# Attention heads as 64x64 tiles of TensorE, and the first activation in one ScalarE instruction

## The chip, the cores and the metric

One core of a Trainium2 chip runs the whole program. A core has TensorE (PE; its weight loads are listed as PEld), VectorE (DVE), ScalarE (ACT), GpSimd (POOL) and the queue that issues most DMAs, SyncE (SP). The metric is device time of one execution in microseconds (us); lower is better.

## The reference

For 8 batches of 8 heads (576 tokens, head width 64) linear attention is computed, then two pairs of dense layers with different activations. The attention's output is rearranged to 4608 tokens of 512 features.

```python
q_s = exp(q - max(q, -1)); q_s /= sum(q_s, -1) + 1e-9      # per token and head
k_s = exp(k - max(k, 2));  k_s /= sum(k_s, 2) + 1e-9       # per head, over its 576 tokens
kv  = einsum('bhsd,bhse->bhde', k_s, v)                    # 64x64 for each head
x   = einsum('bhsd,bhde->bhse', q_s, kv)                   # -> (4608, 512)
h = x @ w_in;   g = h / (1 + exp(-1.702 * h));  x1 = g @ w_out      # 512 -> 2048 -> 512
h2 = x1 @ w2_in; g2 = piecewise quadratic of h2;  out = g2 @ w2_out
```

## The kernel before, in words

A product in full precision is made of three products of rounded parts (high x high, high x low, low x high, type fp32r); `split` (L106) makes the parts: ScalarE copies the high part (L107), VectorE subtracts it (L108).

**Stage 0** is the part that the change touches. It has nine blocks `j` of 512 tokens, each of 16 steps `m`; step `s = 16j + m` is one call of `gemm1` (L794): 12 matmuls of 128x512 (L803 to L805) that give 128 rows of `h` for 512 tokens. Two steps fill a pair of PSUM banks `hps`; there are two such pairs, used in turn. After each second step `act` (L807) takes the pair: ScalarE computes tanh(0.851 h) (L812), VectorE (tanh + 1) * h (L813), which is twice the activation, and SP stores it to `g0` (L816). The factor 0.5 is put into the next stage's copies out of PSUM (`keep`, L396, and `more`, L401).

Beside the steps, `chain` (L824) lays out the attention of the next block. For each of four pairs of heads `hp`: `k_max`, `k_col`, `k_sub` (column maximum by two PE transposes, L681 and L688, and VectorE's subtraction, L691), `k_exp` (L700), and `k_v` (L702): ten fp32 matmuls (each is recorded as two) of a key chunk against [v, 1]; four chunks have 128 rows, the last has 64 (`n = P if r < KR else KT`). The two heads of a pair go to two halves of the array's columns. ScalarE writes the result, divided by the sums, as two 64x64 blocks on the diagonal of a 128x128 tile `kv` (L724); the rest of the tile is zero. For each of four tiles of 128 tokens `t`: `q1`, `q1e`, `q2` (softmax of q, L729 to L755), `q3` (four PE transposes, L764, and a copy, L769), and `q4` (L771): for each pair of heads a 128x128 fp32 matmul `px` per batch that the block reaches into (L774; blocks 1 to 7 reach into two), and `split` of `px` into the parts of `x`.

The first weight matrix is read as 64-bit floats and converted in block 0 itself, one piece `w(m)` of 128 columns for each step: `load_w` (L604), `conv_w` (L610; L92 on ScalarE, L94, L97, L101 on VectorE, then `split`). Later in the stage the other three matrices are converted and stored. **Stages 1 to 3** (`out_pass`, L359; `pass_in`, L485; `out_pass` again) are matmuls on data in DRAM.

What sets the order: the kernel is written as a list of jobs, each with a place in units of steps (`put`, `at`; Q3 and Q4, L46 and L47), sorted and called after each step. The framework then arranges the instructions of each engine by a model of their times, keeping all dependences, and each engine runs its list strictly in order.

## Time and profile before

| what | us |
|---|---|
| time, median of three runs | 1572.76 (1572.35 to 1576.16) |
| the profiled execution's own time | 1570.93 |
| its span, first to last instruction | 1569.1 |
| PE busy in the span | 1536.9 (98%) |
| DVE busy | 1163.6 (74%) |
| ACT busy | 821.9 (52%) |
| first matmul of step 0 begins at | 40.11 |

A busy matmul time counts the tail of a matmul while the next runs already, so what one costs is read from the distance between starts: undisturbed 128x512 matmuls start 0.227 us apart. A window of time shows all engines' busy time in it, the granted clock of TensorE (1.00 is 2.4 GHz, 0.50 is 1.2 GHz) and the load of the DMA engines.

### The profile page before, as it was taken

Reading aid. Unit: us, or ns where it says so; the run is one execution under the profiler, and the core shown is the slowest. Engines: PE = TensorE matmul, PEld = TensorE weight load, DVE = VectorE, ACT = ScalarE, POOL = GpSimd, SP = SyncE. Lnnn points to the kernel's source line nnn. Section 1 sums busy time; section 2 is a strip of 40 time slices with the busy share of each in tenths; the row PEclk is TensorE's granted clock in tenths of the full one; section 3 lists DMA queues with packets and bytes.
Section 4 is the critical chain, followed back from the end, with each engine's and each line's share of the span. In section 5 each row is a group of like instructions: output and inputs, shape, how many; then the busy total and the mean of one; then the engine's idle time right before and its main releaser. Section 6 shows DMA issues by size and latency. Waiting matters only on the chain. (4 is left out here: it accounts for less than half of the span.)

```text
span 1569.1 us, 20971 instructions
## 1 busy us (share of the span) xinstructions
PE 1536.9 (98%) x7748; PEld 1307.6 (83%) x7748; DVE 1163.6 (74%) x1546; ACT 821.9 (52%) x1058; POOL 8.8 (1%) x45
## 2 busy tenths in 40 slices
PE   4999999999999999999999999999999999999998
PEld 2677788777787888888999888888999888888998
DVE  6999887787843678686778577777664879696885
ACT  5555445544523444444445687778776544343442
POOL 0000000000000000000000000000000000000000
PEclk8999999999999999999999999999999999999999
DMA  8787788887787751615268766566744963535341
GB/s 234 212 258 266 263 271 274 267 271 252 251 293 274 289 201 68 213 56 178 71 199 310 294 223 241 202 231 228 259 160 169 426 201 136 159 110 144 111 121 41
DMA packets 249080, 330.65 MB, mean 211 GB/s; under 512 B 129553, under 2 KB 193041, under 8 KB 246289
## 3 DMA queue, kind: packets, MB, share of 16 engines
q1 hardware_dynamic: 243696, 328.09, 62.0%
q10 hardware_dynamic: 5280, 1.21, 0.4%
q8 instruction: 61, 1.00, 0.3%
q14 instruction: 43, 0.34, 0.1%
HBM read 190.84 MB, written 138.41 MB: 210 GB/s over the span
## 5 line engine op out<-in xcount | busy, mean ns | idle before, releaser
L107 ACT ACTIVATE s<-s 128x1024 fp32r<-128x1024 f32 (+2 forms) x363 | 325.1, 901 | 377.9 <-PE z L359 149.7
L108 DVE TENSOR_TENSOR s<-s,s 128x1024 fp32r<-128x1024 f32 (+2 forms) x363 | 369.0, 1023 | 152.7 <-PE zx L359 66.1
L359 PE MATMUL z<-s,w 128*128 128x512 f32 (+1 forms) x1920 | 399.8, 367 | 0.4 <-DVE s L108 0.4
L359 PEld LDWEIGHTS z<-s,w 128*128 128x128 f32 x1920 | 349.5, 188 | 45.9 <-DVE s L108 0.8
L359 PE MATMUL zx<-s,w 128*128 128x512 f32 (+1 forms) x1440 | 300.8, 367 | 0.7 <-DVE s L377 0.7
L359 PEld LDWEIGHTS zx<-s,w 128*128 128x128 f32 x1440 | 262.2, 188 | 34.6 <-DVE s L377 1.0
L803 PE MATMUL hps<-xh,w 128*128 128x512 f32 x576 | 236.2, 410 | 3.0 <-ACT w L107 3.0
L805 PE MATMUL hps<-xh,w 128*128 128x512 f32 x576 | 226.9, 394 | 0.7 <-DVE w L108 0.6
L804 PE MATMUL hps<-xl,w 128*128 128x512 f32 x576 | 226.2, 393 | 0.0
L121 DVE TENSOR_TENSOR s<-s,s 128x1024 f32<-128x1024 f32 (+2 forms) x196 | 204.7, 1058 | 12.7 <-DMA s<-g 8.9
L485 PE MATMUL z<-s,w 128*128 128x512 f32 (+1 forms) x960 | 207.2, 367 | 0.0
L485 PEld LDWEIGHTS z<-s,w 128*128 128x128 f32 x960 | 175.0, 188 | 22.9 <-DVE s L501 0.4
L485 PE MATMUL zx<-s,w 128*128 128x512 f32 (+1 forms) x720 | 158.5, 368 | 1.8 <-DVE s L121 1.6
L485 PEld LDWEIGHTS zx<-s,w 128*128 128x128 f32 x720 | 130.7, 188 | 20.8 <-DVE s L121 3.8
L813 DVE SCALAR_TENSOR_TENSOR sg<-sg,hps 128x1024 f32<-128x1024 f32 x72 | 87.7, 1218 | 62.2 <-ACT sg L812 59.6
L803 PEld LDWEIGHTS hps<-xh,w 128*128 128x128 f32 x576 | 108.8, 189 | 28.8 <-ACT w L107 4.3
L805 PEld LDWEIGHTS hps<-xh,w 128*128 128x128 f32 x576 | 108.2, 188 | 25.6 <-DVE w L108 2.4
L812 ACT ACTIVATE sg<-hps 128x1024 f32<-128x1024 f32 x72 | 73.8, 1025 | 101.4 <-PE hps L805 96.8
L804 PEld LDWEIGHTS hps<-xl,w 128*128 128x128 f32 x576 | 108.5, 188 | 20.9 <-issue 0.6
L500 ACT ACTIVATE s<-s 128x1024 f32<-128x1024 f32 (+1 forms) x80 | 77.6, 971 | 1.6
L499 ACT ACTIVATE s<-s,half 128x1024 f32<-128x1024 f32 (+1 forms) x40 | 42.4, 1060 | 23.6 <-DVE s L121 23.6
L501 DVE SCALAR_TENSOR_TENSOR s<-s,s 128x1024 f32<-128x1024 f32 (+1 forms) x40 | 44.7, 1117 | 12.6 <-ACT s L500 11.2
(79 smaller groups left out, 1074.2 us busy)
## 6 DMA issues: line engine op xcount, KB each, us to landing
s<-g SPq DMA_DIRECT2D x96, 512.0 KB, 5.1
g<-sg SPq DMA_DIRECT2D x72, 512.0 KB, 3.2
w<-wp_out SPq DMA_DIRECT2D x14, 2048.0 KB, 14.8
g<-s SPq DMA_DIRECT2D x48, 512.0 KB, 3.0
s<-g SPq DMA_DIRECT2D x48, 384.0 KB, 4.0
wp_out<-w SPq DMA_DIRECT2D x28, 512.0 KB, 4.0
wp_in<-w SPq DMA_DIRECT2D x28, 512.0 KB, 3.7
w<-wp_in SPq DMA_DIRECT2D x7, 2048.0 KB, 8.7
```

Of the source, the lines that this page charges most:

```text
L107: first = nc.scalar.activation(out=hi, in_=src, func=ACTF.Copy)
L108: return nc.vector.tensor_tensor(out=lo, in0=src, in1=hi.bitcast(FP32), op=ALU.subtract), first
L121: return nc.vector.tensor_tensor(out=o, in0=x, in1=y, op=op)
L359: nc.tensor.matmul(out=z[:, m, :n], lhsT=a, rhs=b[:, c, :], start=(p in OPENS and i == 0 and c == 0 and x == 0), stop=(i == 3 and c == 1 a ...
L485: nc.tensor.matmul(out=z[:, m, :n], lhsT=a, rhs=b[:, c, :], start=(p in OPENS and c == 0 and x == 0), stop=(c == 1 and x == 2), skip_group ...
L500: nc.scalar.activation(out=t, in_=t, func=ACTF.Square)
L501: nc.vector.scalar_tensor_tensor(out=t, in0=h, scalar=1.0, in1=t, op0=ALU.max, op1=ALU.min)
L803: nc.tensor.matmul(out=hps, lhsT=wh, rhs=xh[:, kk, :], start=(kk == 0), stop=False)
L804: nc.tensor.matmul(out=hps, lhsT=wh, rhs=xl[:, kk, :], start=False, stop=False)
L805: nc.tensor.matmul(out=hps, lhsT=wl, rhs=xh[:, kk, :], start=False, stop=(kk == KD - 1))
L812: nc.scalar.activation(out=sg, in_=hps, func=ACTF.Tanh, scale=0.851)
L813: nc.vector.scalar_tensor_tensor(out=sg, in0=sg, scalar=1.0, in1=hps, op0=ALU.add, op1=ALU.mult)
```

## The change

Four things change in stage 0. (1) `q4` handles two pairs of heads at once: per batch four matmuls of 64x64 tiles, one in each quarter of the array (`tile_position`), for four heads; `kv` holds the 64x64 blocks alone, and the rows of the first weight matrix are loaded in another order (two DMAs instead of one for each piece) so that the features fit. (2) In `k_v` all chunks have 128 rows; the rows that the last one lacks hold zeros (v) and exponentials of the lowest number (k). The result leaves PSUM by one activation instead of two. (3) ScalarE's function `Gelu_apprx_sigmoid` computes h*sigmoid(1.702h) in one instruction, and VectorE's instruction falls away, as do the factors 0.5 later. (4) Exponentials and that function are not in the same table of ScalarE, so the exponentials of two tiles of keys and two of queries are put together (EX), an extra order (`in_turn`) keeps ScalarE from mixing them with activations, and the places of the jobs behind them move (KV, Q3, Q4).

```diff
+    EX = (5, 5, 9, 9)
+    KV = (6, 7, 10, 11)
-    Q3 = (6.5, 8.5, 10.5, 12)
-    Q4 = (12.4, 13.2, 14, 14.8)
+    Q3 = (7.5, 8.5, 11.5, 12.5)
+    Q4 = (13.1, 14)
...
-                after(nc.scalar.activation(out=t, in_=z, func=ACTF.Copy, scale=1.0 if ph else 0.5), True)
+                after(nc.scalar.activation(out=t, in_=z, func=ACTF.Copy), True)
...
-                if ph:
-                    after(tt(t, t, z, ALU.add))
-                else:
-                    nc.vector.scalar_tensor_tensor(
-                        out=t, in0=z, scalar=0.5, in1=t, op0=ALU.mult, op1=ALU.add
-                    )
+                after(tt(t, t, z, ALU.add))
...
-        kv_t = [vpool.tile([P, HP, P], FP32, name=f"kv{i}") for i in range(2)]
+        kv_t = [vpool.tile([P, HP, D], FP32, name=f"kv{i}") for i in range(2)]
...
+            src = w1_in[:, m * P:(m + 1) * P].rearrange("(c k d) f -> c d k f", c=2, k=KD)
+            for c in range(2):
+                nc.sync.dma_start(
+                    out=raw1(m)[c * D:(c + 1) * D].rearrange("d (k f) -> d k f", k=KD), in_=src[c]
+                )
...
+        def in_turn(ins):
+            if st.get("turns"):
+                behind(ins, st.get("turn"))
+            st["turn"] = ins
...
-            nc.scalar.activation(out=kt, in_=kt, func=ACTF.Exp)
+            in_turn(nc.scalar.activation(out=kt, in_=kt, func=ACTF.Exp))
...
-                n = P if r < KR else KT
...
-                        lhsT=kt[:n, r, h, :],
-                        rhs=vt[:n, r, h, :],
+                        lhsT=kt[:, r, h, :],
+                        rhs=vt[:, r, h, :],
...
-            for j in range(2):
-                o = slice(j * D, (j + 1) * D)
-                nc.scalar.activation(out=kv[o, hp, o], in_=pk[o, :D], func=ACTF.Copy, scale=rs[o])
+            nc.scalar.activation(out=kv_t[b % 2][:, hp, :], in_=pk[:, :D], func=ACTF.Copy, scale=rs)
...
-        def q4(j, hp):
-            px = ps_a.tile([P, TB], FP32, tag="a", name="px")
+        def q4(j, pair):
+            px = [ps_a.tile([P, TB], FP32, tag="a", name="px") for _ in range(2)]
             for off, n, b, s in segs(j * TB, TB, S):
-                nc.tensor.matmul(
-                    out=px[:, off:off + n],
-                    lhsT=kv_t[b % 2][:, hp, :],
-                    rhs=st["qT", j][:, hp, off:off + n],
-                    start=True,
-                    stop=True,
-                )
+                for c in range(2):
+                    for r in range(2):
+                        rows = slice(r * D, (r + 1) * D)
+                        nc.tensor.matmul(
+                            out=px[r][c * D:(c + 1) * D, off:off + n],
+                            lhsT=kv_t[b % 2][rows, pair + 2 * c, :],
+                            rhs=st["qT", j][rows, pair + 2 * c, off:off + n],
+                            start=True,
+                            stop=True,
+                            tile_position=(r * D, c * D),
+                            skip_group_check=True,
+                        )
             xh, xl = x_sb[j]
-            split(xh[:, hp, :], xl[:, hp, :], px)
+            for r in range(2):
+                split(xh[:, 2 * pair + r, :], xl[:, 2 * pair + r, :], px[r])
...
-            nc.scalar.activation(out=sg, in_=hps, func=ACTF.Tanh, scale=0.851)
-            nc.vector.scalar_tensor_tensor(
-                out=sg, in0=sg, scalar=1.0, in1=hps, op0=ALU.add, op1=ALU.mult
-            )
+            in_turn(nc.scalar.activation(out=sg, in_=hps, func=ACTF.Gelu_apprx_sigmoid))
...
-                    put(2 * i + 3, k_exp, b, i)
-                    put(2 * i + 5, k_v, b, i)
+                    put(EX[i] + 0.3, k_exp, b, i)
+                    put(KV[i], k_v, b, i)
...
-                put(2 * i + 3.3, q1e, t)
-                put(2 * i + 5.2, q2, t)
+                put(EX[i], q1e, t)
+                put(KV[i] + 0.2, q2, t)
                 put(Q3[i], q3, t)
-                put(Q4[i], q4, j, i)
+                if i < 2:
+                    put(Q4[i], q4, j, i)
...
-        for t in kv_t:
-            nc.gpsimd.memset(t, 0.0)
+            nc.gpsimd.memset(t[KT:, KR, :, :D], 0.0)
```

How this moves instructions is seen in the lists of the engines. The line numbers in the lists of the changed kernel are its own: its L813 to L815 are the three matmuls of `gemm1`, L711 `k_v`, L768 `q3`, L781 `q4`, L684 and L691 the two transposes of `k_max`'s chain, L703 and L746 the exponentials of keys and queries, L822 the activation, L723 the copy of `kv`, L773 that of `q3`, L109 `split`'s first instruction, L94 and L169 conversions of later weights.

PE before, block 3, from the end of step 11 to the start of step 13 (most of the twelve matmuls of step 12 are left out):

```order
L805 MATMUL hps<-xh,w 128x512
L709 MATMUL pk<-v_303,kt 64x65 x10
L803 MATMUL hps<-xh,w 128x512
L804 MATMUL hps<-xl,w 128x512
...
L764 MATMUL pt<-ident,qt 128x128 x4
L774 MATMUL px<-qT,kv_305 128x256
L803 MATMUL hps<-xh,w 128x512
L804 MATMUL hps<-xl,w 128x512
L774 MATMUL px<-qT,kv_304 128x256
```

The same engine in the changed kernel, block 3, from the end of step 13:

```order
L815 MATMUL hps<-xh,w 128x512
L711 MATMUL pk<-v_302,kt 64x65 x10
L711 MATMUL pk<-v_303,kt 64x65 x10
L768 MATMUL pt<-ident,qt 128x128 x8
L813 MATMUL hps<-xh,w 128x512
L781 MATMUL px<-qT,kv_305 64x256 x4
L814 MATMUL hps<-xl,w 128x512
...
L781 MATMUL px<-qT,kv_304 64x256 x4
```

Two `k_v`, two `q3` and the first `q4` now stand together, at the start of step 14, where each stood at a step of its own from step 10 to step 13.

ACT before, block 3, from the tanh after step 9 to the one after step 11 (kv, qT, xh: copies out of PSUM):

```order
L812 ACTIVATE sg<-hps 128x1024
L107 ACTIVATE w<-w 128x512 x3
L724 ACTIVATE kv_304<-pk,rs 64x64 x2
L769 ACTIVATE qT<-pt 128x4x128
L107 ACTIVATE w<-w 128x512
L812 ACTIVATE sg<-hps 128x1024
```

ACT in the changed kernel, block 3, from the activation after step 9 to the one after step 11:

```order
L822 ACTIVATE sg<-hps 128x1024
L723 ACTIVATE kv_304<-pk,rs 128x64
L746 ACT_TABLE_LOAD
L746 ACTIVATE qt<-qt 128x512
L773 ACTIVATE qT<-pt 128x4x128
L94 ACTIVATE w<-w 128x1024
...
L746 ACTIVATE qt<-qt 128x512
L703 ACTIVATE kt<-kt 128x640 x2
L822 ACT_TABLE_LOAD
L822 ACTIVATE sg<-hps 128x1024
```

Between two activations ScalarE now has two loads of a table and four exponentials, with copies and conversions between them; there are 34 loads in the list where there was one.

DVE in the changed kernel, block 0, ahead of the weights of step 8 (kt is `k_sub`, qz and the last qt are `q2`, rs follows `k_v`; L96, L99, L103, L110 are the conversion of w(8) and its `split`):

```order
L721 TENSOR_SCALAR rs<-pk 128x1
L686 TENSOR_REDUCE mc<-pa 128x1
L722 RECIPROCAL rs<-rs 128x1
L753 TENSOR_REDUCE qz<-qt 128x8
L96 TENSOR_SCALAR w<-w 128x512
L757 TENSOR_SCALAR qz<-qz 128x8
L694 TENSOR_TENSOR kt<-kr,pb 128x640
L99 SCALAR_TENSOR_TENSOR w<-w 128x512
L758 RECIPROCAL qz<-qz 128x8
L103 SCALAR_TENSOR_TENSOR w<-w 128x512
L759 TENSOR_TENSOR qt<-qt,qz 128x512
L110 TENSOR_TENSOR w<-w 128x512
```

The first of them waits for the `k_v` that PE has at the start of step 8, and `k_sub` for a transpose that PE has behind it; the weights of step 8 stand behind both.

## Rows read from the trace of the kernel before

**Rows 1.** Windows: block 0 of stage 0, then its blocks 1 to 8.

```profile
core 0: us, PE busy (x) PEld busy (x) DVE busy (x) ACT busy (x) POOL busy (x), PEclk, DMA share, GB/s
40.10:101.30 61.20, 57.56 (x315) 43.22 (x314) 59.41 (x120) 35.59 (x59) 0.80 (x4) 1.00 0.78 234
101.30:523.00 421.70, 421.50 (x2281) 336.18 (x2280) 316.07 (x560) 194.40 (x292) 4.43 (x20) 1.00 0.80 268
```

**Rows 2.** Windows with line L803 alone (four to a step): blocks 0 and 1.

```profile
40.10:101.30 61.20, 27.14 (x65) 12.26 (x65) 1.00 0.78 234
101.30:156.00 54.70, 26.88 (x64) 12.15 (x64) 1.00 0.79 259
```

**Rows 3.** Timeline of PE: one q4 (start us, length us, line, tiles).

```profile
201.75 0.39 PE L804 MATMUL hps<-xl,w 128*128 128x512 f32 x1
201.97 0.39 PE L805 MATMUL hps<-xh,w 128*128 128x512 f32 x1
202.20 1.02 PE L774 MATMUL px<-qT,kv 128*128 128x192 f32 x4
202.82 0.63 PE L803 MATMUL hps<-xh,w 128*128 128x512 f32 x1
203.29 0.40 PE L804 MATMUL hps<-xl,w 128*128 128x512 f32 x1
```

**Rows 4.** Timeline of PE: one k_v.

```profile
248.15 0.39 PE L804 MATMUL hps<-xl,w 128*128 128x512 f32 x1
248.37 0.39 PE L805 MATMUL hps<-xh,w 128*128 128x512 f32 x1
248.69 0.95 PE L709 MATMUL pk<-v,kt 128*64 128x65 f32 x20
249.57 0.50 PE L803 MATMUL hps<-xh,w 128*128 128x512 f32 x1
249.91 0.39 PE L804 MATMUL hps<-xl,w 128*128 128x512 f32 x1
```

**Rows 5.** Groups by line and shape, blocks 1 to 8: k_v (count | busy us, mean ns).

```profile
L709 PE MATMUL pk<-v,kt 128*64 128x65 f32 x384 | 18.1, 228 | 0.0
L709 PE MATMUL pk<-v,kt 64*64 64x65 f32 x96 | 8.0, 243 | 0.0
```

**Rows 6.** Waits of PE in block 0 (total us, times, longest).

```profile
PE hps L803 <- ACT w L107: 3.0, 4, 1.2
PE hps L805 <- DVE w L108: 0.6, 1, 0.6
```

**Rows 7.** Timeline of PE: q4 before block 0, and the first matmuls.

```profile
34.41 6.26 PE L774 MATMUL px<-qT,kv 128*128 128x512 f32 x8 [0.88 <-ACT qT L769]
40.11 0.79 PE L803 MATMUL hps<-xh,w 128*128 128x512 f32 x1
```

**Rows 8.** Window of that time, all engines: the granted clock is behind POOL.

```profile
26.00:39.50 13.50, 9.94 (x54) 5.78 (x51) 9.54 (x27) 8.75 (x20) 0.00 (x0) 0.50 0.82 230
```

**Rows 9.** Timeline of ACT: the one load of a table.

```profile
9.36 1.28 ACT L745 ACT_TABLE_LOAD   x1 [9.36 <-DMA qt<-in_q_dram]
10.65 0.63 ACT L745 ACTIVATE qt<-qt 128x512 f32<-128x512 f32 x1
```

**Rows 10.** Groups by line and shape, whole span (count | busy us, mean ns).

```profile
L813 DVE SCALAR_TENSOR_TENSOR sg<-sg,hps 128x1024 f32<-128x1024 f32 x72 | 87.7, 1218 | 62.2 <-ACT sg L812 59.6 <-DMA wp_in<-w 1.6 <-DMA g<-sg 0.9
L812 ACT ACTIVATE sg<-hps 128x1024 f32<-128x1024 f32 x72 | 73.8, 1025 | 101.4 <-PE hps L805 96.8 <-DMA g<-sg 4.2
L724 ACT ACTIVATE kv<-pk,rs 64x64 f32<-64x64 f32 x64 | 19.6, 307 | 23.9 <-DVE rs L720 19.6 <-DVE qz L753 3.9
L691 DVE TENSOR_TENSOR kt<-kr,pb 128x640 f32<-128x640 f32 x32 | 26.2, 817 | 3.8 <-PE pb L688 2.8 <-PE pk L709 0.7
L101 DVE SCALAR_TENSOR_TENSOR w<-w 128x512 uint32<-128x512 uint32 x16 | 10.9, 682 | 0.0
L107 ACT ACTIVATE w<-w 128x512 fp32r<-128x512 f32 x64 | 39.7, 626 | 20.7 <-DVE w L101 8.1 <-DVE w L121 7.5 <-DMA wp_out<-w 3.3
```

More of the change, by code (lines that the diff above doesn't have):

```diff
@@ L604, in load_w @@
         def load_w(m):
-            nc.sync.dma_start(
-                out=raw1(m).rearrange("p (k f) -> p k f", k=KD),
-                in_=w1_in[:, m * P:(m + 1) * P].rearrange("(k p) f -> p k f", p=P),
-            )
+            src = w1_in[:, m * P:(m + 1) * P].rearrange("(c k d) f -> c d k f", c=2, k=KD)
[3 more added lines that the diff above has]
+                )
         def conv_w(m):
@@ L720, in k_v @@
             nc.vector.reciprocal(out=rs, in_=rs)
-            kv = kv_t[b % 2]
-            for j in range(2):
-                o = slice(j * D, (j + 1) * D)
-                nc.scalar.activation(out=kv[o, hp, o], in_=pk[o, :D], func=ACTF.Copy, scale=rs[o])
+            nc.scalar.activation(out=kv_t[b % 2][:, hp, :], in_=pk[:, :D], func=ACTF.Copy, scale=rs)
         def q1(t):
@@ L729, in q1 @@
             nc.vector.tensor_reduce(out=mx, in_=qt, axis=AX.X, op=ALU.max)
-            nc.vector.tensor_tensor(out=qt, in0=qt, in1=mx.to_broadcast([P, H, D]), op=ALU.subtract)
+            st["q1", t % 2] = nc.vector.tensor_tensor(
+                out=qt, in0=qt, in1=mx.to_broadcast([P, H, D]), op=ALU.subtract
+            )
         def q1s(t):
@@ L744, in q1e @@
         def q1e(t):
-            nc.scalar.activation(out=q_t[t], in_=q_t[t], func=ACTF.Exp)
+            in_turn(nc.scalar.activation(out=q_t[t], in_=q_t[t], func=ACTF.Exp))
         def q2(t):
@@ L751, in q2 @@
                 z = sm.tile([P, H, 1], FP32, tag="qz", name="qz")
-                nc.vector.tensor_reduce(out=z, in_=qt, axis=AX.X, op=ALU.add)
+                first = nc.vector.tensor_reduce(out=z, in_=qt, axis=AX.X, op=ALU.add)
+                if t % 2 == 0 and t >= NTB:
+                    behind(first, st["q1", 1])
+                    behind(first, st["sub"])
             nc.vector.tensor_scalar(out=z, in0=z, scalar1=EPS, scalar2=None, op0=ALU.add)
@@ L769, in q3 @@
             nc.scalar.activation(out=st["qT", j][:, :, c * P:(c + 1) * P], in_=pt, func=ACTF.Copy)
-        def q4(j, hp):
-            px = ps_a.tile([P, TB], FP32, tag="a", name="px")
+        def q4(j, pair):
+            px = [ps_a.tile([P, TB], FP32, tag="a", name="px") for _ in range(2)]
             for off, n, b, s in segs(j * TB, TB, S):
-                nc.tensor.matmul(
-                    out=px[:, off:off + n],
-                    lhsT=kv_t[b % 2][:, hp, :],
-                    rhs=st["qT", j][:, hp, off:off + n],
-                    start=True,
-                    stop=True,
-                )
+                for c in range(2):
[9 more added lines that the diff above has]
+                            skip_group_check=True,
+                        )
             xh, xl = x_sb[j]
-            split(xh[:, hp, :], xl[:, hp, :], px)
+            for r in range(2):
+                split(xh[:, 2 * pair + r, :], xl[:, 2 * pair + r, :], px[r])
         x_sb = {}
@@ L810, in act @@
             sg = sgp.tile([P, 2, TB], FP32, tag="sg", name="sg")
-            nc.scalar.activation(out=sg, in_=hps, func=ACTF.Tanh, scale=0.851)
-            nc.vector.scalar_tensor_tensor(
-                out=sg, in0=sg, scalar=1.0, in1=hps, op0=ALU.add, op1=ALU.mult
-            )
+            in_turn(nc.scalar.activation(out=sg, in_=hps, func=ACTF.Gelu_apprx_sigmoid))
             nc.sync.dma_start(out=g0_dram[j][m // 2], in_=sg)
@@ L910 @@
                 conv_w(0)
-        for hp in range(HP):
-            q4(0, hp)
+        for i in range(2):
+            q4(0, i)
         for f, a in jobs.get(-1, ()):
@@ L915 @@
                 f(*a)
+        st["turns"] = True
         for s in range(NB * NM):
```

## The prediction

> **What bounds the kernel.** I read the windows first, cut at the borders of stage 0. In its blocks 1 to 8 PE is busy for 421.50 of 421.70 us, DVE for 316, ACT for 194 [rows 1]. So in those blocks only what PE itself runs is worth time, and work taken from DVE is worth nothing as long as nobody waits for it. Block 0 is different: DVE is busy for 59.41 of 61.20 us and PE for 57.56 [rows 1]. With L803 alone as a counter (64 matmuls to a block) block 0 takes 61.2 us and block 1, with the same steps, 54.7 [rows 2]; the 6.5 us between them are time that block 0 loses to the conversion of the first weights, which no other block has. The waits name the same cause: PE waited 3.0 us for ScalarE's half of `split` of a weight and 0.6 for VectorE's [rows 6]. The rest of the 6.5 is in matmuls that end late without a gap in the records. Then the timeline of PE shows what the small fp32 products cost, by the distance of starts, since 128x512 matmuls start 0.227 us apart when nothing disturbs them. Stages 1 to 3 keep their instructions; ten sums out of PSUM change their form at the same size, for which I take nothing.
>
> **q4.** From the matmul at 201.97 to the one at 203.29 there are 1.32 us, two 128x512 matmuls of 0.227 and one `q4` [rows 3]: 0.87 us for two passes of 512 columns, 0.85 ns for a column and pass. Blocks 0 to 7 hold 32 of them for the next block, 27.8 us. The change makes 16 calls, each for two pairs of heads, with four tiles in four quarters of the array. How many tiles stream at once is not shown by this trace for the row halves. For column halves it is: the 20 records of a `k_v`, with 65 columns each, start and end within 0.88 us [rows 4], 44 ns for one, where one alone needs 65 x 0.85 = 55 ns. So two at once are sure; four would take 16 x 0.87 = 13.9 us, two 27.8. I take four, because the second half of the rows needs other rows of the array and other banks of PSUM than the first, while the two column halves, which do overlap, already share their rows.
>
> A group of tiled matmuls also has to be entered and left. A `k_v` costs 249.91 - 248.37 - 2 x 0.227 = 1.09 us [rows 4]; ten pairs of 65 columns at 0.85 ns are 0.55, and the short chunk loses 0.14 (next part), so 0.40 remain for entering and leaving. The list of PE in the changed kernel has 21 groups for the 16 calls, since some are cut in two or more: 8.4 us. In cut groups fewer than four tiles run; that repeats a stretch of 448 columns in block 0 and one of 384 in block 5, two passes each, 0.76 + 0.65 = 1.4. Sum 13.9 + 8.4 + 1.4 = 23.7 against 27.8: -4.1 us. With two at once it is 27.8 + 8.4 = 36.2: +8.4. The Trainium skill's page "TensorEngine Tiling (Array Packing)", section "Key Properties", says that a change of tiling mode drains TensorE and that tiles work independently. By the second half of that the value would be four at once, as taken; by the first a gain shrinks by the number of groups, for which the trace has the 0.40 us above.
>
> **k_v.** PE was busy for 18.1 us with 384 records of full chunks and 8.0 with 96 of the short one [rows 5]: 47 and 83 ns each, 36 ns more for the four short ones of a call, 0.14 us. At 28 calls inside the blocks this is -4.0 us if the shape alone makes the difference, and 0 if it is only the tail of a group. I take -4.0. But the new list cuts nine `k_v` in two by other work, where before five were cut; four more entries at 0.40 cost +1.6. Sum -2.4 us (0 to -4).
>
> **Start and block 0.** Before block 0 four `q4` take from 34.41 to 40.11, 5.70 us [rows 7], at a granted clock of 0.50, the 1.2 GHz level [rows 8]. Two calls with four tiles take half, 2.85, and 0.8 for entering and leaving twice by the price above: the first matmul starts some 2 us earlier, but until the clock rises (it was at the lower level to 39.5, and I expect no earlier rise) it runs at half speed, so 1.3 us are won there. Whether this reaches the end is decided by the weights. In block 0 DVE loses eight instructions of 1.22 us [rows 10], 9.7 us, more than the 6.5 that the block is too long. Against that stands the new order ahead of w(8): PE begins step 8 with a `k_v` (0.88 us, rows 4); behind it on DVE stand its reciprocal, `k_sub` (0.82), and the conversion, of which two instructions of 0.68 follow `k_sub`, then ScalarE's 0.63 [rows 10]. With the four shorter instructions before `k_sub`, some 1.5 us by the nearest row of 0.68 for the longest of them, PE's first matmul of step 8 comes at 0.88 + 1.5 + 0.82 + 1.36 + 0.63 = 5.2 us after PE reached that place, and PE has 0.88 and a few transposes of its own there, by estimate 1.7. So a wait of some 3.5 us at step 8 takes the place of the 3.6 [rows 6], however early PE comes. What remains to be won is 6.5 - 3.6 = 2.9: -2.9 us (between 0 and -7.8, all of the 6.5 and the 1.3).
>
> **ScalarE.** 33 loads of a table are new. One took 1.28 us, and the exponential behind it started 0.01 us after its end [rows 9]: 42.3 us more for ACT; the single copy of `kv` gives back 32 x 0.31 = 9.9 [rows 10]. ACT has 421.70 - 194.40 = 227 us idle in blocks 1 to 8, and the new loads are 5.1 of some 28 in a block. Queued behind them on ACT are the next activation, which frees the PSUM pair that PE needs two steps later, and the copies of `kv`, `qT` and the parts of `x`. Activation and load before step 14 end about when PE gets there: PE needs 4 x 12 x 0.227 = 10.9 us for the four steps, and ACT's list in that stretch holds two loads (2.6), two activations (2.1) and nine or ten others of 0.3 to 1.2. PE's list puts two `k_v` and two `q3` before step 14, so that PE has work there. I take 0.3 us for each of seven blocks, for this and for `q4` that now stands right behind the `k_v` and `q3` whose copies it needs: +2 us. Bounds: 0, and one load of 1.28 in each block, +9. The two DMAs for each weight piece, 16 more on SP, and the changed zeroing by POOL are hidden as now: PE's waits in block 0 name ACT and DVE, no DMA [rows 6]; if that cover failed it would be in the 2.9.
>
> **Sum.** -4.1 - 2.4 - 2.9 + 2 = -7.4. The profiled execution took 1570.93 us (its span 1569.1 and 1.8 around it), so 1563.5; the median of the runs is 1572.76, 1.8 above it, which gives 1565.4. I say 1565.
>
> **Rivals.** (a) *The row halves do not overlap.* Two tiles at once: `q4` +8.4 instead of -4.1, the start gains nothing; 1565.4 + 12.5 = 1578, slower than before. For it: only column halves are shown [rows 4]. Against: nothing in the trace makes row halves share what column halves do not. `q4` stops gaining when fewer than about three tiles run at once: (27.8 - 9.8)/16 = 1.1 us for a call against 0.87 with four and 1.74 with two. (b) *The exchange of tables ends up on the path.* Rows 9 show a load with no activation before it, so they can't show whether ACT must first run empty. If each load costs another 1.03, the length of an activation [rows 10], a group of exponentials grows by 2.1 us, past PE's room before step 14, and `q4` waits for copies as much later: 7 x 2.1 = 15 less the 2 taken: 1578. The Trainium skill's page "ScalarE: Activation LUTs", section "What ACT_TABLE_LOAD costs", gives about 2.66 us for a switch, of which 1.28 is the load, the same as the trace; by its other 1.38 the number would be 7 x 2.8 less 2, 1583. (c) *All waits vanish*: block 0 gives all 6.5, ScalarE's part costs nothing: 1565.4 - 3.6 - 2 = 1560. (d) *The order costs what the array saves*: waits of one load in each block, +9, eat the gain: 1572. For it: the new lists have transposes and what needs them close together.
>
> **Chances.** Forecast 0.45 (1561 to 1569), (a) 0.14, (b) 0.09, (c) 0.2, (d) 0.12. A difference under 0.3% (4.7 us) can't be told from none. Faster than 1568.0: 0.8 of the forecast and all of (c), 0.57 with rounding. Within: the rest of the forecast and (d), some of (a) and (b), 0.23. Slower than 1577.5: the rest, 0.2. The range that leaves out 2 in 10 is 1554 to 1579.
>
> **What would show it.** In the profile after: 64x64 matmuls of L781, 0.87 us and 0.4 for a whole call between the 128x512 matmuls around them, and four records starting within some 10 ns of each other; `k_v` at 0.95 us; 34 table loads of 1.28; block 0 at about 57 to 58 us, still with a wait of PE at step 8 for the weights; no wait of PE for `hps` above 1 us in blocks 1 to 7. The forecast is wrong if a call of `q4` takes over 1.5 us, if PE waits at step 14 of each block, or if block 0 stays at 61.

## The result

The changed kernel takes 1586.15 us (median of four runs, 1584.87 to 1588.17) against 1572.55; the ratio is 1.0085 [1.0064, 1.0107]. It is slower by 13.6 us, where 1565 had been forecast.

The windows of the kernel after, at the borders of its own blocks (block 0, then blocks 1 to 8), answer to [rows 1]:

```profile
38.50:115.90 77.40, 65.11 (x333) 47.26 (x330) 53.13 (x111) 39.39 (x61) 0.80 (x4) 0.87 0.64 168
115.90:536.70 420.80, 414.47 (x2386) 325.00 (x2385) 248.62 (x499) 219.78 (x298) 5.75 (x20) 1.00 0.83 276
```

Stage 0 starts 1.6 us earlier, blocks 1 to 8 are 0.9 us shorter, and block 0 takes 77.4 us instead of 61.2. The whole loss is in block 0. There VectorE was the busy engine before; now it is idle for 24 us, ScalarE for 38, and the DMA engines moved 168 GB/s instead of 234. PE is idle for 12.3 us (3.6 before); that is 8.7 of the 16.2 lost, and the rest is in matmuls that run slower. PE's waits in block 0 (total us, times, longest), for [rows 6]:

```profile
PE pk L711 <- ACT kt L703: 4.3, 1, 4.3
PE hps L813 <- ACT w L109: 4.1, 1, 4.1
PE pt L768 <- DVE qt L759: 3.4, 1, 3.4
```

During each of these the granted clock fell to 0.50 (1.2 GHz) and stayed there for a while; before, it was at 1.00 throughout block 0 [rows 1]. A window of the first such stretch, and PE's timeline in it, where 128x512 matmuls start 0.43 us apart instead of 0.227:

```profile
60.94:67.77 6.83, 6.35 (x24) 4.62 (x26) 3.12 (x6) 2.79 (x5) 0.00 (x0) 0.50 1.14 284
```

```profile
62.64 0.63 PE L814 MATMUL hps<-xl,w 128*128 128x512 f32 x1
63.07 0.63 PE L815 MATMUL hps<-xh,w 128*128 128x512 f32 x1
63.49 0.63 PE L813 MATMUL hps<-xh,w 128*128 128x512 f32 x1
```

The array does what was expected of it. A q4 for two pairs of heads, two segments of a batch each, and a `k_v`, on PE's timeline of the kernel after (for [rows 3, 4]):

```profile
213.66 0.40 PE L815 MATMUL hps<-xh,w 128*128 128x512 f32 x1
213.99 1.24 PE L781 MATMUL px<-qT,kv 64*64 64x192 f32 x16
215.16 0.50 PE L813 MATMUL hps<-xh,w 128*128 128x512 f32 x1
```

```profile
190.35 0.39 PE L815 MATMUL hps<-xh,w 128*128 128x512 f32 x1
190.67 0.80 PE L711 MATMUL pk<-v,kt 128*64 128x65 f32 x20
191.41 0.32 PE L691 MATMUL pb<-ident,mc 128*128 128x128 f32 x1
191.49 0.47 PE L813 MATMUL hps<-xh,w 128*128 128x512 f32 x1
```

From L815 to L813 there are 1.50 us, less 0.227 for L815: 1.27 us for what cost 2 x 0.87 before. So four tiles stream at once, and the loss is elsewhere.

The queue SP works in another order too. Its timeline before (start us, length of the issue, line, tiles), around the first store of an activation, `g<-sg`:

```profile
32.41 0.52 SPq L633 DMA_DIRECT2D kr<-in_k_dram  x1
...
34.94 0.97 SPq L605 DMA_DIRECT2D w<-in_moe_w_in_dram  x2
...
38.07 0.54 SPq L664 DMA_DIRECT2D qt<-in_q_dram  x1
48.97 0.35 SPq L816 DMA_DIRECT2D g<-sg  x1
```

and after:

```profile
25.12 5.13 SPq L604 DMA_DIRECT2D w<-in_moe_w_in_dram  x4
30.30 1.29 SPq L639 DMA_DIRECT2D v<-in_v_dram  x2
46.34 0.35 SPq L823 DMA_DIRECT2D g<-sg  x1
...
48.10 0.69 SPq L636 DMA_DIRECT2D kr<-in_k_dram  x1
48.84 0.63 SPq L640 DMA_DIRECT2D kr<-in_k_dram  x1
49.56 1.27 SPq L604 DMA_DIRECT2D w<-in_moe_w_in_dram  x2
```

A store waits for its activation, and SP works its list in order. Before, the loads of the next block's third pair of keys (32.41) and of the weight pieces 6 and 7 (34.94) had been issued when SP came to that wait. After, the store stands in front of them: SP issues nothing from 31.6 to 46.3, the keys come 15.7 us later and piece 6 14.6. The lists with which the two kernels were built have the store at the same places.

But no wait of PE, VectorE or ScalarE for a piece of these weights, a key or a query is left in block 0 of the kernel after. Before, there was one, of ScalarE for weight pieces (total us, times, longest, from 40 to 90 us):

```profile
ACT w L92 <- DMA w<-in_moe_w_in_dram: 2.7, 2, 1.7
```

Nor does a half take longer from its issue to its landing than a whole piece, in these kernels (the last number is the median in us; first before, then after):

```profile
w<-in_moe_w_in_dram SPq DMA_DIRECT2D x16, 512.0 KB, 4.9
w<-in_moe_w_in_dram SPq DMA_DIRECT2D x30, 256.0 KB, 4.6
```

What PE waits for is an instruction that stands late in ScalarE's list. The third wait, with what ScalarE ran ahead of it (L94 is the conversion of a piece of the first weights as well as of later ones):

```profile
65.48 2.91 SPq L604 DMA_DIRECT2D w<-in_moe_w_in_dram  x2
85.23 1.02 ACT L822 ACTIVATE sg<-hps 128x1024 f32<-128x1024 f32 x1 [2.18 <-PE hps L815]
86.15 0.65 ACT L94 ACTIVATE w<-w 128x512 f32<-128x512 f32 x1
88.64 0.61 ACT L109 ACTIVATE w<-w 128x512 fp32r<-128x512 f32 x1
89.31 0.80 PE L813 MATMUL hps<-xh,w 128*128 128x512 f32 x1 [4.12 <-ACT w L109]
```

Piece 10 is needed at step 10. Both its halves have landed by 71.8, but its conversion (86.15) stands behind the fifth activation (85.23), which takes steps 8 and 9, so it can't begin before step 9 has ended; then come VectorE's part and `split` (88.64), and PE stands for 4.12 us. Before, the same conversion stood behind three activations.

At the other two waits PE's list has a `k_v` and transposes ahead of the matmuls, so that these name keys and queries. The first one is again ScalarE's: the exponential (L703) and the conversion of piece 6 stand behind the third activation, which takes steps 4 and 5; `split` of this piece begins at 61.27, and PE goes on at 61.42. The second one, at step 8, is the wait that had been forecast: a `k_v` at 71.21, then VectorE's list without a gap, `split` of piece 8 at 76.31, and the first matmul of the step at 77.06. So the trace names the places of instructions in the lists of ScalarE and VectorE, not a transfer.

This is what a trace can tell; which part of the change did it took experiments. Each below was timed in rounds with the kernel before, whose median was 1570.1 to 1572.1 in these.

### The profile page after: what moved, and what is told of

It is laid out like the page before. It is cut to its first block, busy times and chain, and to the rows that moved or that the text cites. A ratio compares the mean times of both kernels' runs of the same rounds, so it can differ in the third digit from the quotient of the medians.

```text
span 1584.6 us, 21113 instructions
## 1 busy us (share of the span) xinstructions
PE 1535.8 (97%) x7876; PEld 1299.0 (82%) x7876; DVE 1087.7 (69%) x1474; ACT 848.3 (54%) x1059; POOL 10.2 (1%) x47
## 5 line engine op out<-in xcount | busy, mean ns | idle before, releaser
L109 ACT ACTIVATE s<-s 128x1024 fp32r<-128x1024 f32 (+2 forms) x363 | 324.9, 901 | 376.8 <-PE zx L361 145.4
L110 DVE TENSOR_TENSOR s<-s,s 128x1024 fp32r<-128x1024 f32 (+2 forms) x363 | 368.9, 1022 | 195.7 <-PE zx L361 65.7
L813 PE MATMUL hps<-xh,w 128*128 128x512 f32 x576 | 235.0, 408 | 4.1 <-ACT w L109 4.1
L814 PE MATMUL hps<-xl,w 128*128 128x512 f32 x576 | 229.4, 398 | 0.0
L815 PE MATMUL hps<-xh,w 128*128 128x512 f32 x576 | 229.0, 398 | 0.0
L123 DVE TENSOR_TENSOR s<-s,s 128x1024 f32<-128x1024 f32 (+2 forms) x196 | 204.5, 1056 | 11.2 <-DMA s<-g 7.1
L822 ACT ACTIVATE sg<-hps 128x1024 f32<-128x1024 f32 x72 | 73.9, 1026 | 124.0 <-PE hps L815 103.6
L813 PEld LDWEIGHTS hps<-xh,w 128*128 128x128 f32 x576 | 110.4, 192 | 36.2 <-issue 6.1
L815 PEld LDWEIGHTS hps<-xh,w 128*128 128x128 f32 x576 | 110.0, 191 | 24.8 <-DVE w L110 1.0
L109 ACT ACTIVATE w<-w 128x512 fp32r<-128x512 f32 x64 | 40.1, 630 | 39.4 <-DVE w L103 28.5
L110 DVE TENSOR_TENSOR w<-w 128x512 fp32r<-128x512 f32 x64 | 43.6, 685 | 16.4 <-ACT w L109 16.1
```

What stands on the lines that cost most here:

```text
L109: first = nc.scalar.activation(out=hi, in_=src, func=ACTF.Copy)
L110: return nc.vector.tensor_tensor(out=lo, in0=src, in1=hi.bitcast(FP32), op=ALU.subtract), first
L123: return nc.vector.tensor_tensor(out=o, in0=x, in1=y, op=op)
L813: nc.tensor.matmul(out=hps, lhsT=wh, rhs=xh[:, kk, :], start=(kk == 0), stop=False)
L814: nc.tensor.matmul(out=hps, lhsT=wh, rhs=xl[:, kk, :], start=False, stop=False)
L815: nc.tensor.matmul(out=hps, lhsT=wl, rhs=xh[:, kk, :], start=False, stop=(kk == KD - 1))
```

## The experiments

**The order of the exponentials, or something else.** My first theory was that the paired exponentials and ScalarE's new order made the loss. `tiles_tanh` keeps of the change the tiles, the full chunk, the single copy and the cut loads of the weights; function, exponentials and places of the jobs are those of before.

```diff
-            in_turn(nc.scalar.activation(out=sg, in_=hps, func=ACTF.Gelu_apprx_sigmoid))
+            in_turn(nc.scalar.activation(out=sg, in_=hps, func=ACTF.Tanh, scale=0.851))
+            nc.vector.scalar_tensor_tensor(...)
-                    put(EX[i] + 0.3, k_exp, b, i)
+                    put(2 * i + 3, k_exp, b, i)
...
```

> The changed kernel with its tiles and its full key chunk, but with the first activation as it was (tanh on ScalarE, then VectorE), the exponentials where they were (2i+3 and 2i+3.3), k_v at 2i+5, and no order laid on ScalarE; one table load in the whole list. Theory 1: the loss comes from the order of the exponentials in pairs, behind which k_v and q3 now wait on PE in block 0, and from TensorE's clock, which falls to 1.2 GHz after such waits. Then this kernel has no wait of several us in block 0, block 0 takes at most 61 us, a call of q4 costs 1.24 us as in the changed kernel, and the total is 1562 to 1569 (before 1572.5, less 4 to 10). Rival 3: the tiles, the doubled weight loads or the full key chunk cost time: then it is 1578 or more. Rival 2 (the table loads themselves): as theory 1, about 1566.

Measured 1602.09, 1.019 [1.017, 1.0209]: slower than the whole change.

`tanh_pairs` is the changed kernel with tanh and VectorE's instruction, but exponentials in pairs:

> The changed kernel with tanh and VectorE's instruction back, but exponentials still in pairs and in turn with the activations: the order without the table loads and without the relief of VectorE. Theory 1 (order): most of the loss stays: block 0 above 66 us, k_v or q3 waiting on PE for exponentials, total 1574 to 1588. Rival 2 (the 33 loads of 1.28 us): the loss is gone, total at most 1570, block 0 at most 62.

Measured 1589.21, 1.0104 [1.0089, 1.0119]. `gelu_free` is the changed kernel without the extra order (`st["turns"] = True` left out):

> The changed kernel without the order laid on ScalarE (in_turn off): the framework places exponentials and activations as it sees fit, and the list has 74 table loads instead of 34. Theory 1 (order): block 0 waits less, 62 to 70 us, total 1566 to 1580 although 40 more loads (51 us of ScalarE) are run. Rival 2 (loads): slower than the changed kernel, 1595 or more, by 40 times 1.28 us as far as ScalarE is in the way.

Measured 1588.19, 1.0092 [1.0073, 1.0111]. That is in neither range: the first theory wanted at most 1580, the theory of the table loads at least 1595, and 40 more table loads change nothing that can be told beside the 1586.15. `gelu_alone` is the other half, the kernel before with ScalarE's function, pairs and order, without tiles, full chunk and cut loads:

> The kernel before with the new activation, the exponentials in pairs and in turn and the later places of k_v and q3 alone (34 table loads); no 64x64 tiles, no full key chunk, single weight loads; q4 at 13.1, 13.4, 14 and 14.8 so that it stands behind q3. Theory 1 and rival 2: slower than the changed kernel by what tiles save, 1588 to 1598, block 0 at 74 to 80 us. Rival 3 (tiles): as before or faster, at most 1574.

Measured 1575.10, 1.002 [1.0009, 1.0031]. The first theory falls: the pairs and the function alone cost 3.0 us, clear of none but a small part of the loss, and every slow kernel has the tiles or what belongs to them.

**The cut load alone.** `split_alone` is the kernel before with this edit and no other (the order of the rows is the old one):

```diff
-            nc.sync.dma_start(out=raw1(m).rearrange(...), in_=w1_in[...].rearrange("(k p) f -> p k f", p=P))
+            src = w1_in[:, m * P:(m + 1) * P].rearrange("(k c d) f -> c d k f", c=2, k=KD)
+            for c in range(2):
+                nc.sync.dma_start(out=raw1(m)[c * D:(c + 1) * D].rearrange(...), in_=src[c])
```

> The kernel before, in which only the load of each piece of the first weights is cut into two DMAs of 64 partitions (rows in the old order). Theory S (SP's list: with 16 more DMAs in it the first stores of activations come to stand ahead of loads of keys, queries and weights that stood ahead of them before, and the loads wait for an activation): block 0 at 72 to 79 us, idle SP from about 31 to 46 us, about 1586 (1580 to 1592). Theory D (DMAs of 64 partitions carry less in a time, whatever the order): also slow, 1578 to 1590. Theory T (the loss comes from the tiles, the full chunk or the new order on PE and DVE): as before, 1572.

Measured 1601.05, 1.019 [1.0175, 1.0206]: +29 us by the load alone, more than the whole change loses. By its trace against that of before, 0.9 of these are a later start, 15.9 are in block 0 (77.1 us against 61.2), and 13.9 in blocks 1 to 8 (435.7 against 421.8), where no half is loaded any more; what costs there stays open. PE's waits for ScalarE's half of `split` are 11.2 us in its block 0, with 3.4, 3.6 and 2.7 at steps 6, 8 and 10. `before_split_pool` adds to it that POOL issues the stores (`nc.gpsimd` for `nc.sync`), and `before_stores_pool` has this alone:

> The same two DMAs of 64 partitions for each piece, and the stores of activations issued by POOL, so that nothing on SP waits for an activation. Theory S: block 0 back at 55 to 62 us, 1566 to 1573. Theory D: still slow, 1578 to 1590. Theory T: as before.

> The kernel before with the stores of activations issued by POOL, one DMA for a piece. It is the control for the run with two: Theory S expects the same as with two DMAs, 1566 to 1573; Theory D expects 8 us or more below the run with two DMAs. By both, if the stores cost the loads something in the kernel before too (its first store stood on SP from 38.6 to 49.0 us ahead of a load of keys), up to 6 us below 1572.

Measured 1589.56, 1.0109 [1.0091, 1.0127], and 1572.27, 1.0006 [0.9996, 1.0016]. With no store on SP's list 11.5 of the 29 us go; 17.3 remain against the control. By the times both S and D would hold in part: the place of the store, and a load that is slow in itself. The traces bear out neither as the path. In `before_split_pool` pieces 6 to 15 had landed 9 to 19 us before their conversions began, and no wait of PE, VectorE or ScalarE in block 0 names one of them. `stores_pool` is the changed kernel with that edit:

> The changed kernel with the stores of activations issued by POOL. Theory S: block 0 goes from 77.4 to 58 to 62 us, the three falls of the clock in it are gone, 1568 to 1572. Theory D: block 0 stays over 70, 1580 or more. Theory T: no change, 1586.

Measured 1573.24, 1.0008 [0.9993, 1.0023], 12.9 us back, as the difference of 11.5 says. Neither range held (S: at most 1572, D: at least 1580). Block 0 is at 68.3 us in its profile, which caught an execution of 1578.98. What the move of the stores gives is thus measured, but not by which path: it changed ScalarE's list as well (the table below).

**As many DMAs, cut the other way.** `split_by_k` also has two DMAs of 256 KB for a piece, but each writes all partitions:

```diff
+            for k in (0, 2):
+                nc.sync.dma_start(out=dst[:, k:k + 2], in_=src[:, k:k + 2])
```

> The kernel before with two DMAs for each piece of the first weights, as many and as large (256 KB) as in the changed kernel, but cut by chunks of rows, so that each still writes all 128 partitions. So far two DMAs of 64 partitions cost 29 us in the kernel before and 17 with the stores on POOL. Theory W (what costs is that a DMA writes only half of the partitions): no loss, block 0 at 60 to 63 us, 1570 to 1576. Theory N (the number of DMAs on SP costs, each with its issue): as with the other cut, 1590 to 1601.

Measured 1570.64, 0.9988 [0.9977, 1.0000]: no loss. Theory N is out; 16 more issues on SP cost nothing. In its list of SP the first store stands behind the same loads as before, so that not their number moved the store either.

What goes with the loss is the place of the conversions in ScalarE's list. For the pieces that are needed at steps 6, 8 and 10 of block 0, the number of activations that stand ahead of the conversion, and for pieces 6 to 15 the time from landing to conversion, all from the traces:

| kernel | us | piece 6 | piece 8 | piece 10 | landing to conversion, us |
|---|---|---|---|---|---|
| before | 1572 | 0 | 2 | 3 | 0.1 to 7.9 |
| `before_stores_pool` | 1572 | 0 | 2 | 3 | 0.1 to 7.8 |
| `split_by_k` | 1571 | 0 | 2 | 3 | 0.1 to 5.2 |
| `split_alone` | 1601 | 3 | 4 | 4 | 2.6 to 11.2 |
| `before_split_pool` | 1590 | 2 | 4 | 4 | 9.0 to 19.0 |
| changed kernel | 1586 | 3 | 4 | 5 | 4.0 to 14.3 |
| `stores_pool` | 1573 | 3 | 3 | 4 | 8.7 to 16.9 |

In the four kernels with halves on SP the data lie ready while ScalarE's list keeps them waiting; in the other three most are converted soon after they come. The pieces share four buffers, so that a late conversion also holds back the load of the piece four later. The lists are made by the framework from modelled times. That its model takes a transfer to 64 partitions for slower is what these lists suggest; no run shows it. No run has halves with the old lists either, so what the chip's own rate for halves would cost there stays open; the runs with two queues, below, come nearest.

The windows 8:40 and 40:100 (columns as in [rows 1]; share of the DMA engines and GB/s are the last two), of before:

```profile
8.00:40.00 32.00, 18.36 (x110) 10.96 (x111) 23.36 (x64) 21.21 (x62) 1.08 (x4) 0.79 0.88 243
40.00:100.00 60.00, 56.36 (x309) 42.17 (x308) 58.21 (x118) 35.70 (x59) 0.80 (x4) 1.00 0.78 234
```

of `split_alone`:

```profile
8.00:40.00 32.00, 18.65 (x109) 11.27 (x110) 23.29 (x64) 20.48 (x60) 1.08 (x4) 1.00 0.83 190
40.00:100.00 60.00, 49.63 (x251) 36.74 (x250) 46.69 (x92) 26.54 (x43) 0.80 (x4) 0.86 0.64 161
```

of `before_split_pool`, where nothing on SP waits for an activation:

```profile
8.00:40.00 32.00, 18.29 (x112) 11.29 (x112) 23.12 (x63) 20.68 (x61) 1.08 (x4) 1.00 0.98 221
```

and of `split_by_k`:

```profile
8.00:40.00 32.00, 19.12 (x112) 11.59 (x113) 23.31 (x63) 21.88 (x63) 1.08 (x4) 1.00 0.84 225
```

GB/s divided by the share gives what the DMA engines move when busy: 276 before and 268 with the other cut, but 229 and 226 with halves. In `before_split_pool` they are busy 0.98 of the first 32 us and still move less than before at 0.88. Its stage 0 starts no later for it, at 39.8 us instead of 40.1.

**The load by itself.** `loads_alone` loads 12 pieces four times ahead of the kernel before, with nothing else running; `loads_alone2` does it with other cuts.

> The kernel before with 12 pieces of the first weights (6.3 MB) loaded four times ahead of everything, with nothing else running: by 12 DMAs of 128 partitions and 512 KB; by 24 of 64 partitions and 256 KB; by 24 of 128 partitions and 256 KB, cut by chunks; and by 24 of 64 partitions, one half from SP and the other from ACT. The loads are used by nothing, and only the times of these stretches count, not the total. Theory W: at the 276 GB/s for a full share that the kernel before had, the first and the third take 23 us each, the second 30 us or more (in the runs so far the stretches with halves moved 225 to 230 GB/s for a full share of the DMA engines, and about half of their bytes were halves). If the halves cost only by their order in SP's list, all four take the same time. By W1 the fourth is as fast as the first, by W2 as slow as the second.

The windows inside the first two stretches, whole pieces and halves from one queue:

```profile
4.00:16.00 12.00, 0.00 (x0) 0.00 (x0) 0.00 (x0) 0.00 (x0) 0.00 (x0) 1.00 1.09 383
24.00:40.00 16.00, 0.00 (x0) 0.00 (x0) 0.00 (x0) 0.00 (x0) 0.00 (x0) 1.00 1.11 243
```

These 6.3 MB take 16 us at 383 GB/s and 26 at 243, where 23 and at least 30 had been expected: halves are slower by more than was thought, and both are faster. The third and the fourth ran into each other and tell nothing, so a second run had them apart:

> Again 12 pieces loaded four times ahead of everything, used by nothing; in the first such run ACT's halves had started among the DMAs cut by chunks, so that neither was measured alone (whole pieces went at about 385 GB/s, halves from one queue at about 243). Now whole pieces; cut by chunks of rows (128 partitions); halves from SP and ACT, each pair side by side; and quarters of 32 partitions from SP. Only the stretches count. Theory W: chunks at 350 to 390 GB/s, quarters slower than halves, 120 to 200. If the size of a DMA counts and not its partitions: chunks at 243 like halves, quarters at 150 or less. W1 (halves beside each other from two queues): 350 to 390; W2: 243.

Its windows: whole pieces; chunks of rows (the stretch where they flow steadily); halves from two queues; quarters of 32 partitions.

```profile
4.00:16.00 12.00, 0.00 (x0) 0.00 (x0) 0.00 (x0) 0.00 (x0) 0.00 (x0) 1.00 1.09 384
30.00:36.00 6.00, 0.00 (x0) 0.00 (x0) 0.00 (x0) 0.00 (x0) 0.00 (x0) 1.00 1.09 383
44.00:56.00 12.00, 0.00 (x0) 0.00 (x0) 0.00 (x0) 0.00 (x0) 0.00 (x0) 1.00 1.10 271
70.00:84.00 14.00, 0.00 (x0) 0.00 (x0) 0.00 (x0) 0.00 (x0) 0.00 (x0) 1.00 1.03 248
```

All four keep the DMA engines fully busy (a share of 1.03 to 1.10). 128 partitions move 383 GB/s, at 512 as at 256 KB; 64 move 243, two halves from two queues 271. I had expected quarters to be slower still (120 to 200); at 248 they are not. So the rate isn't proportional to the partitions. The Trainium skill's page "SBUF — State Buffer", section "Door 1: The DMA port swizzle", says that the rate depends on how many of the 16 ports the partitions reach, and that the first 64 reach no more of them than the first 32. The trace agrees in this, 243 and 248 beside 383; the page's figures, measured with transfers of 1 MiB, are lower (196, 189 and 328), where here many transfers of 128 to 512 KB are in flight. The Trainium skill's page "DMA: Bandwidth & Descriptors", section "Rules for kernel authors", adds that two transfers to disjoint halves don't run beside each other whatever queue issues them. In the main the trace agrees: 271 from two queues is much nearer to 243 than to 383.

So a slower rate of halves is shown for the load by itself. That it is what made the kernels slower is not: in block 0 of the four kernels with halves on SP neither VectorE nor ScalarE waits for one, nor do PE's matmuls.

**Two queues.** `before_two_queues` and `two_queues` are the kernel before and the changed one with the upper halves issued by POOL (`(nc.sync, nc.gpsimd)[c].dma_start`):

> The kernel before with two DMAs of 64 partitions for each piece, one issued by SP and one by POOL, the stores on SP. SP's list is then as before with 16 DMAs for the weights. Theory W1 (the halves are slow because they follow each other in one queue, and beside each other they reach the old rate): 1570 to 1577, block 0 at 60 to 64. Theory W2 (64 partitions are slow however they are issued): 1584 to 1592, block 0 over 68.

> The changed kernel with the two halves of each piece issued by SP and by POOL, the stores on SP. By W1 the changed kernel loses its 29 us of the split and keeps the rest: block 0 at 54 to 60, 1558 to 1567. By W2 1570 to 1580.

Measured 1581.24, 1.0062 [1.0040, 1.0084], and 1561.92, 0.9935 [0.9916, 0.9954]. The rate of 271 is against W1, but the times are not those of W2 either. 1561.92 lies in the range of W1 (1558 to 1567), 1581.24 between the two (at most 1577, at least 1584). In `before_two_queues` SP's list has half the issues of halves and its first store stands as before, and so nearly do the conversions on ScalarE: 1, 2 and 3 activations stand ahead of pieces 6, 8 and 10. Of its 9.4 us 3.8 are a later start (43.9 instead of 40.1), and block 0 takes 63.9 us. In `two_queues` it is 1, 3 and 4, and the next kernel, with whole pieces, is only 2.4 us faster. So with halves, but without the places that the conversions have in the slow kernels, 9.4 of the 29 us are left in the one case and 2.4 of 26.6 in the other.

**The change without halves.** `one_load` makes the features fit with one DMA for a piece: heads are paired (i, i+4) instead of (2i, 2i+1), so that the rows of the weights keep their old order.

```diff
-            load_tokens(t.rearrange("p r h d -> p h r d"), k[b, 2 * hp:2 * hp + 2], True, nc.sync)
+            load_tokens(t.rearrange("p r h d -> p h r d"), k[b, hp:hp + HP + 1:HP], True, nc.sync)
...
+                for r in range(2):
+                    eng.dma_start(
+                        out=qt[off:off + n, r::2],
+                        in_=q[b, r * HP:(r + 1) * HP, s:s + n, :].rearrange("h p d -> p h d"),
+                    )
...
-                            lhsT=kv_t[b % 2][rows, pair + 2 * c, :],
+                            lhsT=kv_t[b % 2][rows, 2 * pair + c, :],
-                split(xh[:, 2 * pair + r, :], xl[:, 2 * pair + r, :], px[r])
+                split(xh[:, pair + 2 * r, :], xl[:, pair + 2 * r, :], px[r])
```

> The changed kernel with one DMA of 128 partitions for each piece, in the old order of the rows. So that the features still fit, a pair of heads is (i, i+4) instead of (2i, 2i+1): keys and values are loaded in such pairs, the queries by two DMAs that put head i+4 behind head i, and q4 takes the groups 2*pair + c. If the cut of the weights is all that made the changed kernel slow, it is 1586 less 29 or, where not all adds up, what was predicted for it: 1556 to 1567, block 0 at 54 to 60, no fall of the clock in it. If the tiles, the paired exponentials or the table exchanges cost something of their own in block 0, it stays over 1572.

Measured 1559.57, 0.9917 [0.9900, 0.9934]: 26.6 us below the changed kernel, 12.3 below the one before. Its block 0 and blocks 1 to 8, and the one kind of wait of PE in block 0:

```profile
37.70:94.10 56.40, 53.89 (x333) 40.79 (x330) 54.78 (x117) 40.89 (x62) 1.14 (x4) 1.00 0.82 250
94.10:509.50 415.40, 411.77 (x2388) 324.32 (x2387) 242.50 (x493) 218.12 (x296) 4.89 (x20) 1.00 0.83 275
```

```profile
PE hps L814 <- ACT w L109: 2.4, 2, 1.2
```

No wait over 1.2 us is left in block 0, and the clock is at 1.00 throughout.

**Which terms made the gain.** `tanh_one_load` is `one_load` with tanh and VectorE's instruction; `tiles_one_load` has besides that the exponentials and jobs at the places of before.

> The version with one DMA for each piece (1559.6), with the tanh and VectorE's instruction in place of ScalarE's own function, exponentials still in pairs: one load of a table, eight more instructions of 1.22 us on VectorE in block 0. If the exchange of tables costs what was taken for it, +2 us in the blocks, and VectorE's share in block 0 is hidden, 1556 to 1559. If VectorE's relief in block 0 is what counts there, 1562 to 1566.

> The version with one DMA for each piece, with the tanh and the exponentials, k_v and q3 at the places of the kernel before: what is left of the change are the 64x64 tiles, the full last chunk and the single copy. By the terms of the prediction, q4 -4.1 and k_v -2.4 and some 3 us at the start, 1561 to 1564. If the tiles give more than was predicted (blocks 1 to 7 became 7.1 us shorter in the version with one DMA), 1558 to 1561. If the new order is what gave the difference, 1566 to 1570.

Measured 1556.09, 0.9903 [0.9887, 0.9920], and 1557.50, 0.9917 [0.9896, 0.9938]. The three intervals overlap: tiles, full chunk and single copy make the gain, ScalarE's function adds nothing that can be measured. Blocks 0 and 1 to 8 of `tanh_one_load` show why:

```profile
38.00:98.30 60.30, 56.57 (x332) 41.67 (x329) 58.72 (x119) 34.57 (x56) 0.80 (x4) 0.98 0.81 245
98.30:509.10 410.80, 409.36 (x2388) 322.43 (x2387) 311.39 (x561) 181.26 (x269) 3.99 (x20) 1.00 0.83 277
```

With ScalarE's function block 0 is 3.9 us shorter (56.4 against 60.3), and blocks 1 to 8 are 4.6 longer (415.4 against 410.8), 3.2 of these in one wait of PE for exponentials in block 6, behind which the clock falls for a while (the only long wait of `one_load` in these blocks):

```profile
PE pk L712 <- ACT kt L704: 3.2, 1, 3.2
```

`tanh_one_load` has the lowest median of all kernels run.

## Why the prediction was wrong

- **The step that failed** is the last sentence of the part on ScalarE: the two DMAs for each weight piece "are hidden as now: PE's waits in block 0 name ACT and DVE, no DMA [rows 6]". It put the cut of the load at nothing; by itself that cut costs 29 us (`split_alone`), and without it the change gains 13 (`one_load`). What the runs showed in its place: the halves are not hidden, and yet nobody waits for one. With them the lists come out otherwise: ScalarE's has the conversions of pieces 6, 8 and 10 behind 3, 4 and 5 activations instead of 0, 2 and 3. PE stands for 4.3 us at step 6 and 4.1 at step 10, which had not been forecast, beside 3.4 at step 8, which had; and in each of the three waits the clock falls. As issues the two DMAs are hidden, since `split_by_k` has as many and loses nothing. Why the framework moves the conversions is only suggested.
- **Why [rows 6] could not carry it.** PE waits for the last link, ScalarE's half of `split`; the row does not say what that link had waited for. The same view of before has ScalarE waiting 2.7 us for pieces of the weights. And a wait says nothing about how the lists will be arranged. These could be read before the run; for the weights of block 0 the prediction compared only VectorE's list, ahead of w(8), and there it was right.
- **Start and block 0**, -2.9 forecast: +14.6 measured (-1.6 at the start, +16.2 in block 0). Without halves -7.2 (-2.4 and -4.8), near the lower bound given, -7.8. "If that cover failed it would be in the 2.9" was too small by far. The one wait that was priced came as forecast: 3.4 us at step 8 for 3.5, and 5.85 us from the `k_v` to the first matmul for 5.2. It was not the only one, and the fall of the clock in such waits had no price. In `one_load` PE's waits are 2.4 us in all.
- **q4**: four tiles at once was right, and 1.27 us for a call is what was estimated from 0.87 and 0.40. **k_v**: 191.49 - 190.35 - 0.227 = 0.91 us, with a transposition in it, where 0.95 were expected. The sum was too small: blocks 1 to 8 of `tanh_one_load` are 10.9 us shorter, forecast were 6.5 for both. The charge for calls that are cut by other work (16 calls in 21 groups) was not tested by this: in the list of `tanh_one_load` the 16 calls stand in 16 groups.
- **ScalarE**, +2 forecast: 4.6 in blocks 1 to 8, and -3.9 in block 0, where VectorE's relief counts; about nothing in sum. In the changed kernel too there is a wait of 3.6 us for exponentials in block 6.
- **Rivals**: (a) is excluded by the 1.27 us; (b) by the trace after, below, and by `tanh_pairs`, which has one load of a table and is no faster than the changed kernel; (d) by `one_load`, which keeps the new order and gains. (c) is nearest to what `one_load` did, 1559.6 against 1560, but in part by luck: tiles and `k_v` gave 10.9 instead of 6.5, and the order on ScalarE cost 4.6 in blocks 1 to 8 instead of nothing. No rival was about the loads; that the number on the slower side, 1578 in (a) and (b), was passed by 8 us comes of that.

For (b), a load of a table behind an activation: the activation ends at 57.73, the load runs from 57.76 to 59.04, and the exponential starts at 59.05. Neither another 1.03 us nor another 1.38 is there.

```profile
56.71 1.02 ACT L822 ACTIVATE sg<-hps 128x1024 f32<-128x1024 f32 x1 [4.05 <-PE hps L815]
57.76 1.28 ACT L746 ACT_TABLE_LOAD   x1
59.05 0.63 ACT L746 ACTIVATE qt<-qt 128x512 f32<-128x512 f32 x1
```

## What to carry to other kernels

When an edit changes the shape or the number of DMAs, compare the lists of all engines and queues before and after, also of those that the edit doesn't name: here a cut of a load moved instructions of ScalarE. A wait that names a compute engine doesn't say why that engine was late: follow that engine's own wait, either to a transfer or to the instructions ahead of it in its list. Where the data had landed long before they were used, a faster load will not help. And price the bytes of a DMA by rows of transfers with that many partitions; a load that writes all 128 was worth a detour in the layout here, heads paired (i, i+4).

## What was not expected of the hardware

- 32 partitions load as fast as 64: 248 and 243 GB/s beside 383, with the DMA engines fully busy in all three.
- A wait can cost more than its length: in the three waits of 3.4 to 4.3 us in block 0 of the kernel after, the clock fell to 0.50, and behind them matmuls of 128x512 started 0.43 us apart instead of 0.227. The length of a single wait doesn't tell whether it falls: in `split_by_k` it fell at 69.2 us (0.50 from 69.20 to 72.50) behind waits of 1.2, 0.5 and 0.6 us, and the kernel before, with waits of the same lengths at nearly the same times, stayed at 1.00.
